# Opening of a windowed-attention and MLP-mixer kernel: loads in smaller pieces, earlier casting DMAs, wider zero matmuls, another mask on TensorE

## The chip, the cores and the metric

The kernel runs on one core of a Trainium2 chip. The metric is the device time of one execution in microseconds. Its engines run beside each other, each with its own queue: TensorE (PE; its weight loads are listed apart as PEld), VectorE (DVE), ScalarE (ACT), GpSimd (POOL) and SyncE (SP), which here only issues DMAs. Sixteen DMA engines move the data of all queues.

## What is computed

The input is q, k and v of 4 batches with 8 heads, 768 positions and 64 channels per head. Attention sees the first 4 positions (the sinks) and a window of 128; the result goes through a mixer of two small networks, one over positions ("token") and one over channels.

```
scores = scale * (q @ k^T);  pos = arange(S);  rel = pos[:, None] - pos[None, :]
keep = (pos[None, :] < n_sink) | ((rel >= 0) & (rel < window))        # 4 and 128
scores = where(keep, scores, -1e9);  a = softmax(scores);  x = a @ v   # heads side by side: [4, 768, 512]
h = relu(x^T @ w_tok1) @ w_tok2                                       # over the 768 positions
u = x + h^T
out = u + relu(u @ w_ch1) @ w_ch2                                     # 512 -> 1536 -> 512 channels
```

## The kernel before

The work is cut into operations (`Op`), each with the engines that may do it, an estimated duration, and what it depends on. A planner, `order_of`, puts them in order with a list-scheduling rule, and each engine's instructions are emitted in that order. For the opening the order is written out by hand in `FIRST`: each word is an operation and its engine (`:P` TensorE, `:D` VectorE, `:A` ScalarE, `:G` GpSimd, `:S` SyncE). Every engine works its own list strictly in order and waits where its next instruction's inputs are missing.

There are eight groups, each of four heads of one batch. A group goes through these steps:

- **L, load.** Group 0's q and k come as fp32 by SyncE's DMAs (`plain`, L355) in `PIECES[0]` pieces each, and are cast to bf16 by ScalarE or VectorE (`C`, L234). All later groups' q and k come by GpSimd's DMAs, which cast on the way (`casting`, L363). v comes by SyncE (L373) and is cast later (`Cv`, L232 or L233).
- **T, turn.** VectorE transposes q and k in 32x32 blocks (L395).
- **SC, scores** (L447). A block `u` of 256 keys (three per group) against up to 512 queries. For groups 0 and 1 two heads go together, each on 32 rows of the array, into one of two PSUM slots of two banks (kind "sc").
- **EX, exponentials** by ScalarE from PSUM (L464), which frees the slot.
- **MK, mask.** VectorE multiplies by 0 and 1 (L475, with `mfirst` and `mrest`), except for the (group, block) pairs in `PEM`: there TensorE first writes -30000 where a key is not seen (`ident` times `mneg`, L440) and adds the scores onto it.
- **KZ, SK, EXK.** The sink keys, spread over heads with `blk`, their scores (L501) and exponentials (L506).
- **PV** (L520 for the sinks, L523 and L528 for the window) and **XB** (L543, L544: divide by the sum).

Once both groups of a batch are through, the mixer follows: T1 (L572, needs `w_tok1`), H1, TT and T2 (L603 to L624), U, X, C1 (L657), V, C2 (L679) and the output's addition and store (L689, L694). While C1 and C2 of one batch run, the planner mixes in the next batch's attention.

The weights come by GpSimd's DMA queue, in a fixed sequence; the first of them, w_tok1, is not issued before group 0's v has landed. The queue also carries the sink rows of v (`vsl`, L307) and waits for earlier DMAs when eight are under way.

Where the planner sees a gap before a TensorE operation, `Filler.make` puts matmuls of zeros there, up to 29 us of its own time: at the very start matmuls of 512 columns over 128 rows (L791), in later gaps matmuls of 128 columns, over 32 rows ahead of scores (L793), over 128 rows otherwise.

Of the kernel before, what the change touches and what calls it, by code (L numbers as in the profile page):

```python
# [16 lines left out]


FIRST = """
warm:D ones:D va:G Lk0.1:S kz:D Lq0.0:S blk:G Lk0.0:S zero:D vsink:A ident:G Lq0.1:S Lv0.0:S mneg:G Lv1.0:S  # L20
Lv1.1:S Ck0.1:A Lk1.0:G mnegs:D Tk0.1:D Lq1.0:G Cq0.0:A vs1:G Tq0.0:D Ck0.0:A vsl:G Tk0.0:D Cq0.1:A Tq0.1:D
first:G KZ0:D SC0.22:P rest:G first1:D SK0:P EX0.21:A Tk1.0:D SC0.20:P SC0.10:P EX0.20:A EX0.10:A SC0.12:P
MK0.20:D EX0.11:A SC0.02:P KZ1:D Tq1.0:D EXK0:A SC0.00:P Wtok1:G EX0.01:A Wtok2:G EX0.00:A Cv0:D SC1.00:P
SK1:P Wch1.0:G EX1.00:A MK0.10:D PV0.5:P PV0.1:P Wch1.1:G PV0.0:P EXK1:A SC1.02:P XB0.5:D Cv1:G SC1.12:P
EX1.01:A XB0.0:D PV0.4:P XB0.1:D PV0.2:P EX1.11:A Wch1.2:G XB0.4:D SC1.10:P PV0.3:P MK1.00:D EX1.10:A Wch1.3:G
SC1.20:P XB0.2:D Wch2.0:G XB0.3:D SC1.22:P EX1.20:A MK1.0256:D Wch2.1:G T10.010:P EX1.21:A MK1.10:D PV1.0:P
PV1.1:P T10.000:P T10.004:P XB1.0:D PV1.2:P H10.00:A PV1.3:P PV1.4:P XB1.2:D PV1.5:P T10.014:P XB1.4:D
T10.110:P H10.01:A T10.100:P T10.104:P T10.114:P H10.10:D TT0.01:P H10.11:D TT0.00:P UE0.01:A TT0.02:P
UE0.00:A TT0.03:P UE0.02:A UE0.03:A C10.03:P C10.02:P V0.03:A C10.00:P V0.02:D C10.01:P V0.00:D V0.01:D
"""  # L30


# [7 lines left out]
class Op:  # L40


    n = 0
# [23 lines left out]
def order_of(ops, slots, filler):  # L67

    free_at = {e: 0.8 for e in ("PE", "ACT", "DVE", "POOL", "SP")}
    banks = {kind: [0.0] * n for kind, n in slots.items()}  # L70
    dma_free, rows = {"SP": 1.9, "POOL": 6.0, "ACT": 1.9}, None
    port = 0.0
    flying = {"SP": [0.0] * 8, "POOL": [0.0] * 8}
    flying["ACT"] = flying["SP"]
    for o in reversed(sorted(ops, key=lambda o: o.seq)):
        for d in o.deps:
            d.far = max(d.far, o.far + min(o.engines.values()) + (0.2 if "PE" in d.engines else 0.07))
    waiting = sorted(ops, key=lambda o: o.seq)
    done = []

    def start(op, e):
        t = free_at[e]
        for d in op.deps:
            t = max(t, d.end + lag(d, op, e))
        for d in op.follows:
            t = max(t, d.begin + d.engines[d.engine])
        if op.take:
            for kind in {p.kind for p in op.take}:
                n = sum(p.kind == kind for p in op.take)
                t = max(t, sorted(banks[kind])[n - 1])  # L90
        if op.dmas:
            t = max(t, flying[e][-9 + op.dmas])
        if e in op.port:
            t = max(t, port)
        if e == "PE" and op.rows != rows:
            t += 0.095
        return t

    while waiting:
        best = None  # L100
        ready = [o for o in waiting if all(d.end is not None for d in o.deps + o.follows)]
        per = {}
        for o in ready:
            at = {e: start(o, e) for e in o.engines}
            soonest = min(at[e] + o.engines[e] + o.dear.get(e, 0) for e in at)
            for e, t in at.items():
                if t < INF and t + o.engines[e] + o.dear.get(e, 0) <= soonest + 1e-9:
                    per.setdefault(e, []).append((t, o))
        for e, c in per.items():
            first = min(t for t, _ in c)  # L110
            t, o = min(((t, o) for t, o in c if t <= first + 0.2), key=lambda x: (x[1].pri, -x[1].far, x[1].seq))
            if best is None or t < best[0]:
                best = (t, e, o)
        if best is None:
            raise RuntimeError("stuck: " + ", ".join(o.name for o in waiting[:20]))
        t, e, o = best
        idle = t - free_at["PE"] - (1.0 if rows is None else 0.15)
        kind, i = min(((k, i) for k in banks for i in range(slots[k])), key=lambda x: banks[x[0]][x[1]])
        if e == "PE" and filler.until > t and idle > 0.15 and banks[kind][i] < free_at["PE"] - 0.2:
            f = filler.make(kind, i, idle, rows is None, o.rows)  # L120
            f.begin, f.engine = free_at["PE"], "PE"
            f.end = banks[kind][i] = f.begin + f.engines["PE"]
            done.append(f)
        o.begin, o.engine = t, e
        free_at[e] = t + o.engines[e]
        if e in o.port:
            port = free_at[e]
        if e == "PE":
            rows = o.rows
        if o.land:  # L130
            dma_free[e] = max(dma_free[e], t + (2.8 if e == "POOL" else 1.4)) + o.land
            o.end = dma_free[e] + 0.9
            flying[e] += [o.end] * o.dmas
        else:
            o.end = free_at[e]
        for p in o.take:
            p.slot = min(range(len(banks[p.kind])), key=lambda i: banks[p.kind][i])
            banks[p.kind][p.slot] = INF
        for p in o.free:
            p.left -= 1  # L140
            if p.left == 0:
                banks[p.kind][p.slot] = free_at[e] + 0.07
        done.append(o)
        waiting.remove(o)
    return done
# [11 lines left out]
def kernel(  # L157
# [13 lines left out]
    nc = tc.nc  # L171
    B, H, S, D = q.shape
    P = 128
# [13 lines left out]
    Q = 32  # L187
# [21 lines left out]
    ident = singles.tile([P, P], BF16, name="ident")  # L209
# [15 lines left out]
    def op(name, engines, emit, deps=(), pri=0, **kw):  # L225
        if not isinstance(engines, dict):
            engines = dict([engines])
        o = Op(name, engines, emit, deps, pri, **kw)
        ops.append(o)
        return o  # L230
# [46 lines left out]
    def c_masks(m):  # L277
        def emit(e):
            z = m.rearrange("p (x c q) -> p x c q", c=2, q=P)
            causal(nc.gpsimd, z[:, :, 0], 0.0)  # L280
            behind(nc.gpsimd, z[:, :, 1], 0.0)
        return emit
# [41 lines left out]
        pass  # L324

    groups = [Group() for _ in range(NG)]
    PEM = ((0, 0), (1, 2))
    PIECES = (2, 1, 1, 1, 1, 1, 1, 1)
    PAIRS = (1,)
    BW, BWV = 0.37, 0.25  # L330

    def behind_of(ins, o):

# [47 lines left out]
    def attention(g, xb, base):  # L381
        G = groups[g]
# [7 lines left out]
        def turn(w, c):  # L390
            def emit(e):
                if w not in G.T:
                    G.T[w] = att.tile([P, S, 2], BF16, name=w + "T")
                r = ts(c, S // Q // C)
                nc.vector.transpose(  # L395
                    G.T[w].rearrange("p s x -> p (s x)").bitcast(UINT32).rearrange("p (i r) -> p r i", i=Q)[:, r],
                    G.bf[w][:, r].bitcast(UINT32))
            old = (prev.sc + [prev.sk]) if prev else []
            return op(f"T{w}{g}.{c}", ("DVE", 2.0 / C + 0.1), emit, G.load[w][c:c + 1] + old, early + c)

        dts = {"q": [], "k": []}
        for c in range(C):
# [309 lines left out]

    o_warm = op("warm", ("DVE", 0.27), c_warm, (), -200)
    o_table = op("table", ("ACT", 1.4), c_table, [o_warm], -60)
    c_ident_op = op("ident", ("POOL", 1.1), c_ident, (), -200)
    o_zero = op("zero", ("DVE", 0.5), c_zero, (), -199)
    o_mneg = op("mneg", ("POOL", 1.4), c_mneg, [o_zero], -199)
    c_mneg_op = op("mnegs", ("DVE", 0.17), c_mneg_sink, [o_mneg], -199)
# [6 lines left out]
    load_ops(0, [], [], -250)  # L725
    load_ops(1, [], [], -180)
    for o in groups[1].load["q"] + groups[1].load["k"]:
        o.deps += [c_ident_op, o_mneg, c_blk_op]
    o_vs1 = op("vs1", ("POOL", 0.9), c_vsink_one, [o_vs], -151)
    c_vsink_op = op("vsl", ("POOL", 2.6), c_vsink_load, [o_vs1], -150, land=2.0)  # L730
    c_vsink_op.dmas = 4
    o_first = op("first", ("POOL", 0.65), c_masks(mfirst), [o_ones], -120)
    c_first_op = op("first1", ("DVE", 0.17), c_mfirst_sink, [o_first], -120)
    c_rest_op = op("rest", ("POOL", 0.65), c_masks(mrest), [o_ones], -119)

    def weight(key, dst, src, deps, pri, run):

# [40 lines left out]
    class Filler:  # L778
# [2 lines left out]
        until = 29.0  # L781

        @staticmethod
        def make(kind, i, us, first, rows):
            n = int(us / 0.33) if first else int(us / 0.058)

            def emit(e):
                t = psum[kind][i].tile([P, 512], FP32, name="ps_warm", tag="b")
                for _ in range(n):
                    if first:  # L790
                        nc.tensor.matmul(t, warm[:, 0:P], warm, start=True, stop=True)  # L791
                    elif rows:
                        nc.tensor.matmul(t[:, 0:P], warm[0:Q, 0:P], warm[0:Q, 0:P], start=True, stop=True, tile_position=(0, 0))  # L793
                    else:
                        nc.tensor.matmul(t[:, 0:P], warm[:, 0:P], warm[:, 0:P], start=True, stop=True)
            return Op("dummy", {"PE": us}, emit)

    with tc.manual_schedule():
# [35 lines left out]
```

## Time and profile before

| | us |
|---|---|
| median of 8 runs | 220.37 |
| fastest and slowest of them | 219.42, 221.60 |
| the profiled execution | 220.16 |
| its span, first to last instruction | 218.5 |
| TensorE busy | 205.8 (94%) |
| VectorE busy | 127.8 (58%) |
| ScalarE busy | 107.1 (49%) |
| GpSimd busy | 32.4 (15%) |

The span starts with the first instruction. The page's chain is the sequence of work and waits that ended last, followed back from the end; the idle time of an engine is put down to what released it, inferred from semaphores. The page also has a row of 40 slices for each engine, of 5.46 us each, with the clock that TensorE was granted and the share of the DMA engines:

```profile
PE   7799999999889699999989999999999999999994
ACT  8485733733856224788652330598553301753300
PEclk9965999999999999999999999999999999999999
DMA  6999999999999955540000112200001112101122
```

The first digit of each row is the slice from 0 to 5.46 us; 9 means nine tenths or more. The costliest groups are the mixer's matmuls (columns: line, engine, operation, tiles, shapes and count, then busy time and mean in ns, then idle time of the engine before them):

```profile
L657 PE MATMUL ps_v<-uT,w_ch 128*128 128x384 bf16 x384 | 68.2, 326 | 0.4
L679 PE MATMUL ps_w<-w_ch,v 128*128 128x512 bf16 (+1 forms) x288 | 64.7, 370 | 0.6
L464 ACT ACTIVATE pT<-ps_s 128x1024 bf16<-128x1024 f32 (+1 forms) x48 | 43.6, 952 | 26.4 <-PE ps_s L447 24.7
L447 PE MATMUL ps_s<-qT,kT 32*128 32x256 bf16 (+1 forms) x384 | 20.4, 279 | 2.3 <-DVE kz L419 1.6
```

### The profile page before, as it was taken

The page shows a single profiled execution, that of the slowest core. Times are in us where ns is not written, and L with a number is a line of the kernel's source. Part 1 is how long each engine was busy: PE and PEld are TensorE (multiplying, and loading weights), DVE is VectorE, ACT ScalarE, POOL GpSimd, SP SyncE. Part 2 cuts the span into 40 slices and gives each one's busy share as a digit, 9 for nine tenths or more (in the row PEclk, how much of TensorE's full clock was granted, in tenths as well). Part 3 has the DMA queues.
Part 4 walks back from the last instruction along what each step waited for, and adds up shares of the span by engine and source line. Part 5 has one row for each costly group of instructions (what it writes and reads, how often), then busy time and mean ns, then how long its engine had stood idle before and what let it go on. Part 6 is the DMA issues. An engine that isn't in the chain of part 4 may idle for free.

```text
span 218.5 us, 4156 instructions
## 1 busy us (share of the span) xinstructions
PE 205.8 (94%) x1748; PEld 117.9 (54%) x1767; DVE 127.8 (58%) x227; ACT 107.1 (49%) x176; POOL 32.4 (15%) x54
## 2 busy tenths in 40 slices
PE   7799999999889699999989999999999999999994
PEld 2346685655455465565735554466665545655543
DVE  4767865199698998989999212588471122001132
ACT  8485733733856224788652330598553301753300
POOL 7709700002633030111000000000000000000000
PEclk9965999999999999999999999999999999999999
DMA  6999999999999955540000112200001112101122
GB/s 200 249 220 175 202 203 200 208 231 218 216 221 252 233 145 117 104 91 0 3 0 0 51 48 96 98 3 3 0 3 48 48 48 99 48 1 48 48 99 96
DMA packets 36243, 23.89 MB, mean 109 GB/s; under 512 B 26112, under 2 KB 30976, under 8 KB 36224
## 3 DMA queue, kind: packets, MB, share of 16 engines
q1 hardware_dynamic: 28896, 14.16, 26.0%
q0 software_dynamic: 7328, 9.46, 25.0%
q8 instruction: 14, 0.23, 0.4%
q14 instruction: 5, 0.04, 0.1%
HBM read 26.77 MB, written 6.29 MB: 151 GB/s over the span
## 4 chain that ended last, share of the span: by engine, by line
PE 77%; DVE 10%; DMA 6%; ACT 3%; issue 2%; SPq 1%; POOLq 0%; POOL 0%
PE ps_v L657 26%; PE ps_w L679 26%; PE ps_s L447 6%; PE ps_u L624 5%; PE ps_h L572 4%; DVE pT L475 3%; DMA qb<-in_q_dram 3%; DMA raw_q<-in_q_dram 3%; DVE x_b L544 3%; DVE qT L395 2%; ACT pT L464 2%; PE ps_ut L634 2%; PE ps_k L501 2%; PE ps_o L523 2%; PE ps_o L520 2%
## 5 line engine op out<-in xcount | busy, mean ns | idle before, releaser
L657 PE MATMUL ps_v<-uT,w_ch 128*128 128x384 bf16 x384 | 68.2, 326 | 0.4
L238 ACT ACTIVATE v<-ps_v 128x384 bf16<-128x384 f32 x85 | 41.4, 494 | 50.8 <-PE ps_v L657 40.0
L679 PE MATMUL ps_w<-w_ch,v 128*128 128x512 bf16 (+1 forms) x288 | 64.7, 370 | 0.6
L464 ACT ACTIVATE pT<-ps_s 128x1024 bf16<-128x1024 f32 (+1 forms) x48 | 43.6, 952 | 26.4 <-PE ps_s L447 24.7
L689 DVE TENSOR_TENSOR o<-ps_w,u_sb 128x512 f32<-128x512 f32 (+1 forms) x25 | 16.7, 672 | 59.2 <-PE ps_w L679 59.2
L657 PEld LDWEIGHTS <-w_ch 128*128 128x128 bf16 x384 | 36.4, 98 | 25.6 <-DVE x_b L544 0.8
L679 PEld LDWEIGHTS <-v 128*128 128x128 bf16 x300 | 28.8, 98 | 30.2 <-issue 0.4
L475 DVE TENSOR_TENSOR pT<-pT,mrest 128x2048 bf16<-128x2048 bf16 (+2 forms) x22 | 22.2, 1021 | 0.9 <-ACT pT L464 0.7
L447 PE MATMUL ps_s<-qT,kT 32*128 32x256 bf16 (+1 forms) x384 | 20.4, 279 | 2.3 <-DVE kz L419 1.6
L629 DVE TENSOR_TENSOR u_sb<-ps_u,x_b 128x512 bf16<-128x512 f32 x24 | 15.2, 684 | 9.6 <-PE ps_v L657 5.1
L544 DVE TENSOR_TENSOR x_b<-ps_o,rc 128x256 bf16<-128x256 f32 (+1 forms) x45 | 19.9, 442 | 1.6
L395 DVE STREAM_TRANSPOSE kT<-kb 128x768 uint32<-128x768 uint32 (+1 forms) x9 | 16.8, 1870 | 3.6 <-DMA kb<-in_k_dram 2.3
L447 PEld LDWEIGHTS <-kT 32*128 32x128 bf16 x384 | 11.1, 97 | 12.4 <-issue 9.7
L523 PE MATMUL ps_o<-va,pT 128*128 128x65 bf16 x192 | 16.8, 197 | 1.1 <-DVE v L240 0.8
L395 DVE STREAM_TRANSPOSE qT<-qb 128x768 uint32<-128x768 uint32 (+1 forms) x9 | 16.6, 1871 | 1.2 <-DMA qb<-in_q_dram 0.9
L233 POOL CAST va<-raw_v 128x1536 bf16<-128x1536 f32 x7 | 10.7, 1523 | 44.2 <-DMA raw_v<-in_v_dram 22.5
L523 PEld LDWEIGHTS <-pT 128*128 128x128 bf16 x192 | 14.3, 100 | 2.5 <-DVE pT L475 0.8
L528 PE MATMUL ps_o<-va,pT 128*128 128x65 bf16 x160 | 15.2, 196 | 0.0
L234 ACT ACTIVATE uT<-ps_ut 128x512 bf16<-128x512 bf16 (+1 forms) x14 | 7.9, 567 | 10.0 <-PE ps_ut L634 8.3
L572 PE MATMUL ps_h<-x_b,w_tok 128*128 128x256 bf16 x96 | 12.3, 273 | 0.2 <-DVE x_b L544 0.2
L624 PE MATMUL ps_u<-h,w_tok 128*128 128x512 bf16 x44 | 12.2, 378 | 0.3 <-ACT uT L234 0.2
L528 PEld LDWEIGHTS <-pT 128*128 128x128 bf16 x160 | 11.6, 100 | 0.8 <-issue 0.4
(63 smaller groups left out, 135.9 us busy)
## 6 DMA issues: line engine op xcount, KB each, us to landing
out_dram<-o SPq DMA_DIRECT2D x23, 256.0 KB, 2.0
raw_v<-in_v_dram SPq DMA_DIRECT2D x7, 768.0 KB, 12.9
kb<-in_k_dram POOLq DMA_DIRECT2D x7, 384.0 KB, 11.4
qb<-in_q_dram POOLq DMA_DIRECT2D x7, 384.0 KB, 9.3
w_ch<-in_moe_w_ch_dram POOLq DMA_DIRECT2D x4, 384.0 KB, 8.5
w_ch<-in_moe_w_ch_dram POOLq DMA_DIRECT2D x1, 1024.0 KB, 14.4
raw_k<-in_k_dram SPq DMA_DIRECT2D x2, 384.0 KB, 4.3
raw_q<-in_q_dram SPq DMA_DIRECT2D x2, 384.0 KB, 5.0
```

The lines of the kernel that those rows point to most:

```text
L238: nc.scalar.activation(o, i, AF.Relu)
L395: nc.vector.transpose(G.T[w].rearrange("p s x -> p (s x)").bitcast(UINT32).rearrange("p (i r) -> p r i", i=Q)[:, r], G.bf[w][:, r].bitcast ...
L447: nc.tensor.matmul(bank[h][:, at:at + w], G.T["k"][r, ts(kt, P), db], G.T["q"][r, ds(kt * P, w), db], start=not pem and db == 0, stop=db = ...
L464: nc.scalar.activation(o, i, AF.Exp, scale=scale)
L475: nc.vector.tensor_tensor(out=t, in0=t, op=ALU.mult, in1=m[:, 0:hi - lo].rearrange("p (o x) -> p o x", o=1).to_broadcast([P, GH, hi - lo]))
L523: nc.tensor.matmul(ps[:, h], G.pT[qt // 2][:, h, ds(256 * (qt % 2), P)], G.va[:, h, qt], start=(qt < 2 and h == 0), stop=(h == GH - 1 and ...
L528: nc.tensor.matmul(ps[:, h], G.pT[kt // 2][:, h, ds(256 * (kt % 2) + P, P)], G.va[:, h, kt], start=False, stop=(h == GH - 1), skip_group_c ...
L544: nc.vector.tensor_tensor(out=xb.tile[:, ds(q0, n), c0:c0 + W].rearrange("p n (h d) -> p n h d", h=GH), in0=ps[:, :, :, 0:D], in1=rc.to_br ...
L572: nc.tensor.matmul(p.tile, w_tok1[:, t, ts(tt, P)], xb.tile[:, t, ds(a * W, W)], start=(t == 0), stop=(t == NT - 1))
L624: nc.tensor.matmul(ps, w_tok2[:, tt, ts(st, P)], M.h1t[:, tt], start=(tt == 0), stop=(tt == NTOK - 1))
L657: nc.tensor.matmul(ps, w_ch1[:, c, ts(ft, P)], M.uT[hf][:, c], start=(c == 0), stop=(c == NC - 1))
L679: nc.tensor.matmul(p.tile, M.v1t[hf][:, ft, ts(st % NH, P)], w_ch2[:, ft, ds(lo, n)], start=(ft == 0), stop=(ft == NF - 1))
```

## The change

It has five parts.

1. Group 0's q and k come in three pieces each, six DMAs of 256 KB where there were four of 384 KB (`PIECES`). The new order loads and casts q's last piece first; that first cast is VectorE's, the other five are ScalarE's.
2. Group 1's two casting DMAs no longer wait for `mneg`. They stand third in GpSimd's list, after `ident` and `blk`, and q goes ahead of k; `mneg` now follows them, and `va`, `vs1`, `first` and `rest` follow `mneg`.
3. The zero matmuls ahead of the first scores are counted anew (29 where there were 24), and those in later gaps have 256 columns over 128 rows; `idle` is measured with other margins.
4. `PEM` gets the pair (0, 1): group 0's second block is masked by TensorE too, so two of its three blocks are.
5. The planner's figures for the DMA queues, the transposes, `ident` and the load rate are altered, and `FIRST` is written anew with the score blocks of group 0 in another sequence (heads 2 and 3 of all three blocks, then heads 0 and 1). Through the planner this also moves later work: eight C1 matmuls now stand ahead of group 2's scores, and group 4's q is turned after group 3's attention rather than within it.

```diff
 FIRST = """
-warm:D ones:D va:G Lk0.1:S kz:D Lq0.0:S blk:G Lk0.0:S zero:D vsink:A ident:G Lq0.1:S Lv0.0:S mneg:G Lv1.0:S
-Lv1.1:S Ck0.1:A Lk1.0:G mnegs:D Tk0.1:D Lq1.0:G Cq0.0:A vs1:G Tq0.0:D Ck0.0:A vsl:G Tk0.0:D Cq0.1:A Tq0.1:D
-first:G KZ0:D SC0.22:P rest:G first1:D SK0:P EX0.21:A Tk1.0:D SC0.20:P SC0.10:P EX0.20:A EX0.10:A SC0.12:P
-MK0.20:D EX0.11:A SC0.02:P KZ1:D Tq1.0:D EXK0:A SC0.00:P Wtok1:G EX0.01:A Wtok2:G EX0.00:A Cv0:D SC1.00:P
...
+warm:D ident:G Lq0.2:S ones:D vsink:A Lk0.1:S blk:G kz:D Lq0.1:S zero:D Lq1.0:G Lk0.2:S Lk1.0:G Lq0.0:S mneg:G
+Lk0.0:S Lv0.0:S Cq0.2:D Lv1.1:S Tq0.2:D va:G Lv1.0:S Ck0.1:A vs1:G mnegs:D Tk0.1:D Cq0.1:A first:G Ck0.2:A
+Tq0.1:D rest:G Cq0.0:A Tk0.2:D vsl:G Ck0.0:A Tq0.0:D Tk0.0:D KZ0:D SC0.22:P first1:D SC0.12:P EX0.21:A Tq1.0:D
+SC0.02:P EX0.11:A SK0:P EX0.01:A Tk1.0:D SC0.20:P EX0.20:A SC0.00:P EXK0:A SC0.10:P KZ1:D EX0.00:A Cv0:D
+Wtok1:G SK1:P Wtok2:G EX0.10:A MK0.20:D PV0.1:P SC1.02:P Wch1.0:G XB0.1:D EXK1:A SC1.00:P EX1.01:A PV0.0:P
...
-    dma_free, rows = {"SP": 1.9, "POOL": 6.0, "ACT": 1.9}, None
+    dma_free, rows = {"SP": 2.1, "POOL": 6.9, "ACT": 2.1}, None
...
-        idle = t - free_at["PE"] - (1.0 if rows is None else 0.15)
+        idle = t - free_at["PE"] - (0.0 if rows is None else 0.1)
-        if e == "PE" and filler.until > t and idle > 0.15 and banks[kind][i] < free_at["PE"] - 0.2:
-            f = filler.make(kind, i, idle, rows is None, o.rows)
+        if e == "PE" and filler.until > t and idle > 0.2 and banks[kind][i] < free_at["PE"] - 0.2:
+            f = filler.make(kind, i, idle, rows is None)
...
+            t = max(t, f.end + 0.095 * o.rows)
-            dma_free[e] = max(dma_free[e], t + (2.8 if e == "POOL" else 1.4)) + o.land
+            dma_free[e] = max(dma_free[e], t + (3.3 if e == "POOL" else 1.4)) + o.land
...
-    PEM = ((0, 0), (1, 2))
-    PIECES = (2, 1, 1, 1, 1, 1, 1, 1)
+    PEM = ((0, 0), (0, 1), (1, 2))
+    PIECES = (3, 1, 1, 1, 1, 1, 1, 1)
-    BW, BWV = 0.37, 0.25
+    BW, BWV = 0.35, 0.25
...
-            return op(f"T{w}{g}.{c}", ("DVE", 2.0 / C + 0.1), emit, G.load[w][c:c + 1] + old, early + c)
+            return op(f"T{w}{g}.{c}", ("DVE", 1.96 / C + 0.16), emit, G.load[w][c:c + 1] + old, early + c)
...
-    c_ident_op = op("ident", ("POOL", 1.1), c_ident, (), -200)
+    c_ident_op = op("ident", ("POOL", 0.5), c_ident, (), -200)
...
-        o.deps += [c_ident_op, o_mneg, c_blk_op]
+        o.deps += [c_ident_op, c_blk_op]
+    o_mneg.follows = list(groups[1].load["k"])
...
+    for o in (c_va_op, o_vs1, o_first):
+        o.follows = [o_mneg]
+    c_rest_op.follows = [o_mneg]
...
-            n = int(us / 0.33) if first else int(us / 0.058)
+            n, w = (11 + int((us - 4.8) / 0.216), 512) if first else (round(us / 0.11), 256)
...
-                    if first:
-                        nc.tensor.matmul(t, warm[:, 0:P], warm, start=True, stop=True)
-                    elif rows:
-                        nc.tensor.matmul(t[:, 0:P], warm[0:Q, 0:P], warm[0:Q, 0:P], start=True, stop=True, tile_position=(0, 0))
-                    else:
-                        nc.tensor.matmul(t[:, 0:P], warm[:, 0:P], warm[:, 0:P], start=True, stop=True)
+                    nc.tensor.matmul(t[:, 0:w], warm[:, 0:P], warm[:, 0:w], start=True, stop=True)
```

More of the change, by code (lines that the diff above doesn't have):

```diff
@@ L19 @@
 FIRST = """
-warm:D ones:D va:G Lk0.1:S kz:D Lq0.0:S blk:G Lk0.0:S zero:D vsink:A ident:G Lq0.1:S Lv0.0:S mneg:G Lv1.0:S
-Lv1.1:S Ck0.1:A Lk1.0:G mnegs:D Tk0.1:D Lq1.0:G Cq0.0:A vs1:G Tq0.0:D Ck0.0:A vsl:G Tk0.0:D Cq0.1:A Tq0.1:D
-first:G KZ0:D SC0.22:P rest:G first1:D SK0:P EX0.21:A Tk1.0:D SC0.20:P SC0.10:P EX0.20:A EX0.10:A SC0.12:P
-MK0.20:D EX0.11:A SC0.02:P KZ1:D Tq1.0:D EXK0:A SC0.00:P Wtok1:G EX0.01:A Wtok2:G EX0.00:A Cv0:D SC1.00:P
[L24 to L29, printed above, removed]
+warm:D ident:G Lq0.2:S ones:D vsink:A Lk0.1:S blk:G kz:D Lq0.1:S zero:D Lq1.0:G Lk0.2:S Lk1.0:G Lq0.0:S mneg:G
[3 more added lines that the diff above has]
+Wtok1:G SK1:P Wtok2:G EX0.10:A MK0.20:D PV0.1:P SC1.02:P Wch1.0:G XB0.1:D EXK1:A SC1.00:P EX1.01:A PV0.0:P
+Wch1.1:G PV0.4:P XB0.0:D PV0.2:P XB0.4:D EX1.00:A Cv1:G SC1.10:P XB0.2:D PV0.3:P EX1.10:A SC1.12:P XB0.3:D
+Wch1.2:G PV0.5:P MK1.0256:D EX1.11:A SC1.22:P Wch1.3:G XB0.5:D SC1.20:P MK1.00:D Wch2.0:G EX1.21:A MK1.10:D
+T10.000:P Wch2.1:G EX1.20:A PV1.0:P PV1.1:P T10.004:P XB1.0:D PV1.2:P H10.00:A PV1.3:P PV1.4:P XB1.2:D PV1.5:P
+T10.010:P XB1.4:D T10.100:P T10.014:P T10.110:P H10.01:A T10.114:P T10.104:P H10.11:A TT0.00:P H10.10:A
+TT0.01:P UE0.00:D TT0.02:P UE0.01:A TT0.03:P UE0.02:A UE0.03:A C10.03:P C10.00:P V0.03:D C10.01:P V0.00:D
+C10.02:P V0.01:D V0.02:D
 """
@@ L783, in make @@
         @staticmethod
-        def make(kind, i, us, first, rows):
-            n = int(us / 0.33) if first else int(us / 0.058)
+        def make(kind, i, us, first):
+            n, w = (11 + int((us - 4.8) / 0.216), 512) if first else (round(us / 0.11), 256)
             def emit(e):
```

## The prediction

> **What bounds the kernel now.** I read the page first (busy shares, the slices, the chain), then stretches of the span, then the timelines of ScalarE, GpSimd and VectorE over the opening, then the DMA queues by stretch. The page has TensorE busy for 94% of the span and on 77% of the chain, so a microsecond in which TensorE is slow or waits is a microsecond of the kernel. The exception is its clock: the slices show tenths "9965999", so I cut the opening where the granted clock changes (columns: stretch, its length, busy time and instructions of TensorE, its weight loads, VectorE, ScalarE, GpSimd, then clock, DMA share, GB/s):
>
> ```profile
> 5.86:9.27 3.41, 3.00 (x14) 1.26 (x13) 2.45 (x4) 1.82 (x3) 3.33 (x9) 1.00 1.09 269
> 9.27:12.68 3.41, 2.24 (x32) 1.53 (x32) 1.37 (x3) 1.49 (x2) 0.62 (x2) 1.00 1.16 217
> 12.68:16.10 3.42, 3.00 (x28) 1.37 (x26) 3.16 (x4) 2.77 (x5) 0.24 (x1) 0.50 1.23 223
> 16.10:19.51 3.41, 3.41 (x25) 1.82 (x24) 3.41 (x3) 2.03 (x3) 3.41 (x4) 0.50 1.20 169
> 19.51:22.92 3.41, 3.41 (x37) 2.40 (x37) 2.01 (x7) 1.72 (x3) 3.41 (x5) 0.50 1.22 194
> 22.92:26.34 3.42, 3.42 (x57) 2.05 (x53) 2.52 (x8) 3.07 (x4) 2.85 (x5) 1.00 1.31 203
> ```
>
> The clock is halved from 12.68 to 22.92 us, and in these 10.24 us ScalarE, which makes the exponentials, is busy 6.52 us. Its timeline (start, duration, line, tiles, idle time before and its releaser) shows that it waits for TensorE's scores each time:
>
> ```profile
> 8.38 0.84 ACT L234 ACTIVATE qb<-raw_q 128x768 bf16<-128x768 f32 x1 [0.59 <-DMA raw_q<-in_q_dram]
> 10.99 0.81 ACT L464 ACTIVATE pT<-ps_s 128x768 bf16<-128x768 f32 x1 [1.77 <-PE ps_s L447]
> 15.89 1.02 ACT L464 ACTIVATE pT<-ps_s 128x1024 bf16<-128x1024 f32 x1 [0.44 <-PE ps_s L447]
> 17.82 1.02 ACT L464 ACTIVATE pT<-ps_s 128x1024 bf16<-128x1024 f32 x1 [0.91 <-PE ps_s L447]
> 19.31 1.02 ACT L464 ACTIVATE pT<-ps_s 128x1024 bf16<-128x1024 f32 x1 [0.47 <-PE ps_s L447]
> 22.56 3.10 ACT L464 ACTIVATE pT<-ps_s 128x1024 bf16<-128x1024 f32 x3 [1.69 <-PE ps_s L447]
> 25.87 1.69 ACT L464 ACTIVATE pT<-ps_s 128x768 bf16<-128x768 f32 x2 [0.20 <-PE ps_s L447]
> ```
>
> Groups 0 and 1 need four exponentials of 0.81, eight of 1.02 and two of 0.59: 12.6 us. They take from 10.99 to 27.56, 16.6 us; 4.0 us are stalls. After them TensorE is dense: from its first token-mixing matmul (L572, 26.71) to 54.94 it loses about 0.2 us. So the opening is a chain of three: the first q and k, the scores at half clock, the exponentials. The DMA engines are full from 2 to 78 us, yet the weights land before use (first token weight at 21.79, used at 26.71). The chain has one more stall that the change touches:
>
> ```profile
> 59.78 7.24 DMA qb<-in_q_dram
> 67.05 2.09 DVE qT L395
> ```
>
> Here VectorE waits 0.9 us for a later group's q, then turns it, in the middle of group 3's masks.
>
> [...] Weighing each matmul by its columns and its share of the 128 rows, I get 0.30 of full work in 9.27 to 12.68 (clock lost), 0.55 and 0.55 in the next two (not regained), 0.72 in 19.51 to 22.92 (regained); later windows at 0.50 (from 70.7) and 0.53 (from 74.1) keep it. So it is lost somewhere between 0.30 and 0.50, and regained between 0.55 and 0.72. [...] these two stretches (6 to 8.6 us, then 10.5 to 12.5 us) show: once GpSimd's queue has data, both send the same number of packets, 138 and 136, and its large ones take 96% of the engines.
>
> ```profile
> q1 hardware_dynamic: 1534, 0.74, 102.3%
> ...
> q0 software_dynamic: 138, 0.38, 96.1%
> q1 hardware_dynamic: 136, 0.03, 12.6%
> ```
>
> **The change part by part.**
>
> Six pieces. The last 384 KB piece lands at 8.35; then come its cast (0.84), its transpose (1.13) and 0.12 of hand-over: scores at 10.44. With 256 KB the cast is about 0.63 (two thirds of 768 columns and the fixed part) and the transpose 0.82 (0.94 per 12 rows from the forms 1.13 and 2.07, plus 0.19), so the scores follow the landing by 1.6, not 2.09. Two more DMA issues at 0.43 each put the v loads back by 0.9 us in SP's queue; they share the engines with the end of q and k from 6.9 us on now, so that helps slightly. If the last piece still lands near 8.35, the scores can start at 9.95.
>
> Casting DMAs third. They leave GpSimd at about 2.2 us, after ident (0.5) and blk (0.8), not at 4.11. When do they move data? Before, their first packet came at 8.74, 4.6 us after the issue; later single issues on an empty queue took 1.25 (80.33 to 81.58). Bounds for the first packet: 3.5 to 6.8 us. At 6.8 only some 5 of the 48 raw packets per DMA engine are left and each waits for one casting packet of 0.25 us: 1.2 us, landing near 8.4 because v no longer mixes in. I take this, since the 4.6 us is the only first use of that queue in the trace. Group 1's q and k then land near 11 and 12.5 (before: 14.98 and 12.91), their two transposes (2.07) end by about 15.2, not 17.89. The moved GpSimd work (mneg 1.3, va 0.4, vsink 0.9, masks 1.4, four sink DMAs 2.4) ends at about 10 as before; mneg is ready at 4.7, the sinks' DMAs queue behind the casts as before. First v is behind the same bytes: still about 15.5, so w_tok1, which waits for it, still lands near 21.5.
>
> Wide zero matmuls. The opening run grows from 24 to 29. With the clock raised at 5.86, 10.8 run at 0.427 us and 18.2 at 0.216: it ends at 9.8, where the scores start. If the window falls at 8.1 it ends at 10.9, if at 4.7 at 9.2: on average 0.2 us lost. The 19 small ones (L793, a quarter of the rows) go; only one gap of two 256-wide ones is left in the new order.
>
> Masks on TensorE. Group 0's second block: four matmuls of 0.213 at full clock replace VectorE's 1.21 us multiply. TensorE is ahead of ScalarE there, so they cost nothing, unless the clock is down (0.427 each).
>
> The sum, engine by engine, at full clock. Scores 9.9; exponentials from 10.45. Two score banks alternate, each score block (0.45, with a mask 0.9) fits beside an exponential of 1.02: u2 ends at 11.26, u1 12.42, u0 13.44, u2 14.25, sinks 14.84, u0 15.86, u1 16.88. Group 1's keys are ready at 15.3, so its sink scores go at 15.6. The first PV waits for v cast on VectorE (15.6 to 16.6), and group 1's scores stand behind it in TensorE's order: at 17.0, for an exponential that can start at 17.5. Then 0.59 and six exponentials: 23.3. The first L572 matmul goes when the last score block is out, at 22.4, where w_tok1 has landed 0.9 us before. Before: 26.71. Gain 4.3, minus 0.2 for the window's phase.
>
> The window rule on this schedule: about 0.70, 0.61, 0.51 and 0.63 of full work from 9.27 to 22.92. The third is the weak one, at the edge of what was seen to hold.
>
> After 22.4. The new order puts eight first-channel matmuls (1.3 us) ahead of group 2's scores and takes nothing else out, so these come at 52.0, not 54.94. Group 2's k lands at 46.5 and its transpose ends by 48.7; v is cast at 52.4 and used from 55.6: covered by 3 us. Group 4's q is now turned after group 3's attention: at most 1.8 us of TensorE idle time between 66 and 78 goes, but VectorE, nearly full from 57 to 118, gets the 2.09 back before group 4. I take 0.3 of gain (bounds 1.5 gain, 1.0 loss, since the order of three later groups shifts as well).
>
> Profiled run: 220.16 (span 218.5 and 1.7 outside) minus 4.1 minus 0.3 is 215.8. The median is 0.2 above that run: 216.0.
>
> **Rivals.**
>
> *Half the gain.* One of the weak windows falls under the clock's limit, or loads and VectorE take some back between 52 and 118. For: the third window at 0.51, and VectorE at 3.7 to 4.0 of every 4 us from 86 to 114. Against: loads have 3 us to spare. A window of 3.4 us at half clock costs about 2: 218.2.
>
> *Nothing.* All of it is met by the DMA engines, which are full to 78 us: what lands late then holds group 2 and 3. Against: q, k, v of these are used 3 us or more after landing. 220.2.
>
> *Slower: the casting DMAs overtake the first loads.* Place: the DMA engines, 3.5 to 8 us. If their first packet comes before about 5.1 us, at least 16 raw packets per engine are still to go, and all 16 casting packets (0.246 each) step between: 3.9 us more, last piece at 11.3, scores at 12.9. The zero matmuls end at 9.8, so the window to 12.7 holds under 0.2 of full work and the clock goes. Masked score blocks at half clock take 1.7, 0.7 more than an exponential; with one such window the exponentials end at 28.1, with two at 30, against 27.56. That is 221 to 223, say 222. It decides from a landing of about 10.4 us on. For: single issues had data after 1.25 us. Against: the 4.6 us at this very place.
>
> **How the numbers follow.** Full gain 0.50 (own range 214.3 to 217.6), half 0.21, nothing 0.10, slower 0.19. What a measurement of this kernel can tell from no change is about 0.5%, that is 219.3 to 221.5. Full and half are faster, 0.71, with a little of "nothing" 0.72; same 0.10; slower 0.18, as a mild case of the last falls within. The range from 214.3 to 221.2 leaves out some 0.05 below and 0.15 above.
>
> **What would show it.** Right: last raw piece landing by 8.6; first exponential at 10.5; a clock of 1.00 from 6 us on; ScalarE without stalls over 0.3 us to 23; first L572 at 22 to 23; group 2's scores near 52. Wrong: casting packets before 5 us and a raw landing past 10; a half clock anywhere before 23; a first L572 after 25; VectorE or TensorE idle time over 7 us after it.

## The result, and the profile after

The kernel after takes 222.65 us (median of 11 runs, 221.04 to 223.34); the kernel before, timed beside it, 220.34 (32 runs). The ratio is 1.009, 95% interval 1.0065 to 1.0115: 0.9% slower, a small loss but clear of the interval, where 216.0 was forecast. Here and below, ratios leave disturbed executions out and medians don't, so some medians (x4, x9) lie above what their ratios say. The profiled execution took 221.08, its span 219.4, against 218.5 before.

First the opening, cut where the granted clock changes (columns: stretch, length, busy time and count of TensorE, weight loads, VectorE, ScalarE, GpSimd, then clock, DMA share, GB/s):

```profile
6.15:9.56 3.41, 3.41 (x17) 1.53 (x16) 1.59 (x4) 0.63 (x1) 3.27 (x7) 1.00 1.08 249
9.56:12.98 3.42, 0.53 (x3) 0.04 (x1) 1.83 (x3) 1.89 (x3) 0.00 (x0) 1.00 1.20 258
12.98:16.39 3.41, 2.73 (x19) 1.02 (x20) 3.38 (x5) 0.81 (x1) 0.00 (x0) 0.50 1.36 211
16.39:19.80 3.41, 3.07 (x21) 1.06 (x20) 2.62 (x3) 2.05 (x2) 3.23 (x4) 0.50 1.07 151
19.80:23.22 3.42, 3.42 (x20) 0.98 (x14) 1.36 (x1) 2.05 (x3) 3.42 (x5) 0.50 1.27 200
23.22:26.63 3.41, 3.41 (x59) 2.38 (x60) 1.26 (x5) 2.93 (x5) 3.03 (x5) 1.00 1.32 204
```

In the second stretch TensorE has work for 0.53 of 3.42 us, and three stretches of 3.41 us at half clock follow, as before; such a stretch is called a window here and in the prediction. In both traces the granted clock changes a whole number of windows behind the moment at which the zero matmuls begin to follow each other in 0.22 us instead of 0.43: after at 12.98, 23.22 and 217.78 us, behind 6.15; before at 12.68, 22.92 and 217.48, behind 5.86. TensorE's timeline says what it waited for (start, duration, line, tiles, idle time before and its releaser):

```profile
1.26 8.83 PE L796 MATMUL ps_warm<-warm 128*128 128x512 bf16 x29 [1.26 <-DVE warm L256]
13.66 0.82 PE L449 MATMUL ps_s<-qT,kT 32*128 32x256 bf16 x8 [3.57 <-DVE kT L397]
```

The zero matmuls end at 10.09, and the first scores stand 3.57 us behind them, waiting for the last piece of k. ScalarE's timeline follows k back to its DMA and on to the exponentials:

```profile
7.75 0.63 ACT L236 ACTIVATE qb<-raw_q 128x512 bf16<-128x512 f32 x1 [2.92 <-DMA raw_q<-in_q_dram]
10.31 0.63 ACT L236 ACTIVATE kb<-raw_k 128x512 bf16<-128x512 f32 x1 [1.93 <-DMA raw_k<-in_k_dram]
11.23 0.63 ACT L236 ACTIVATE qb<-raw_q 128x512 bf16<-128x512 f32 x1 [0.30 <-DMA raw_q<-in_q_dram]
12.13 0.63 ACT L236 ACTIVATE kb<-raw_k 128x512 bf16<-128x512 f32 x1 [0.26 <-DMA raw_k<-in_k_dram]
14.52 0.81 ACT L466 ACTIVATE pT<-ps_s 128x768 bf16<-128x768 f32 x1 [1.76 <-PE ps_s L449]
16.45 1.02 ACT L466 ACTIVATE pT<-ps_s 128x1024 bf16<-128x1024 f32 x1 [1.12 <-PE ps_s L449]
18.39 1.02 ACT L466 ACTIVATE pT<-ps_s 128x1024 bf16<-128x1024 f32 x1 [0.91 <-PE ps_s L449]
```

The last raw piece lands at 12.10 us; before, at 8.35. The first exponential is 3.5 us later (14.52, before 10.99), and the stalls of half clock are still there (1.12, 0.91). The DMA queues from 6 to 8.6 us, the stretch that before held SyncE's packets alone (queue, packets, MB, share of 16 engines):

```profile
q0 software_dynamic: 141, 0.39, 77.0%
q1 hardware_dynamic: 136, 0.25, 29.9%
```

GpSimd's queue sends packet for packet with SyncE's (141 and 136), and its packets, 0.23 us each against 0.09, take 77% of the engines just while q and k of group 0 should come in. Its first packet moves at 4.94 us.

The loss shrinks later. The first token-mixing matmul (T1 below: L574, L572 before) starts at 30.24 us, 3.6 later than before (26.64), but the span is only 0.9 longer: from T1 to the end it takes 189.2 us instead of 191.9. Group 4's q is now turned at 79.51, without a wait. The slices and the costliest groups hardly differ:

```profile
PE   7859999999989999989999999999999999999993
ACT  7236874353496613698744730496553301753300
PEclk9965899999999999999999999999999999999998
DMA  6999999999999916391000012200001113001122
```

```profile
L466 ACT ACTIVATE pT<-ps_s 128x1024 bf16<-128x1024 f32 (+1 forms) x48 | 43.8, 953 | 14.3 <-PE ps_s L449 12.2
...
L449 PE MATMUL ps_s<-qT,kT 32*128 32x256 bf16 (+1 forms) x384 | 20.0, 276 | 4.6 <-DVE kT L397 3.6
```

In the slices the half clock reaches further into the fifth one. Of the groups one number is new: the 3.6 us in which TensorE waited for `kT`. ScalarE's idle time before its window exponentials fell from 26.4 to 14.3 us, but most of that only moved: 10.4 us now stand before the sinks' exponentials (L508), where there were none.

### The profile page after: what moved, and what is told of

Read it like the earlier page. It is cut to its first block, busy times and chain, and to the rows that moved or that the text cites. A ratio compares the mean times of both kernels' runs of the same rounds, so it can differ in the third digit from the quotient of the medians.

```text
span 219.4 us, 4147 instructions
## 1 busy us (share of the span) xinstructions
PE 206.2 (94%) x1738; PEld 116.7 (53%) x1759; DVE 128.0 (58%) x229; ACT 107.3 (49%) x177; POOL 31.7 (14%) x54
## 4 chain that ended last, share of the span: by engine, by line
PE 85%; DMA 4%; DVE 4%; ACT 3%; issue 2%; SPq 1%; ACTq 0%
PE ps_w L681 28%; PE ps_v L659 28%; PE ps_s L449 8%; PE ps_h L574 5%; PE ps_u L626 5%; DMA raw_k<-in_k_dram 4%; PE ps_o L525 2%; PE ps_s L442 2%; PE ps_o L522 2%; PE ps_ut L636 2%; ACT pT L466 2%; PE ps_o L530 2%; DVE pT L477 1%; DVE x_b L546 1%; PE ps_k L503 1%
## 5 line engine op out<-in xcount | busy, mean ns | idle before, releaser
L240 ACT ACTIVATE v<-ps_v 128x384 bf16<-128x384 f32 x87 | 42.6, 493 | 50.0 <-PE ps_v L659 39.0
L466 ACT ACTIVATE pT<-ps_s 128x1024 bf16<-128x1024 f32 (+1 forms) x48 | 43.8, 953 | 14.3 <-PE ps_s L449 12.2
L477 DVE TENSOR_TENSOR pT<-pT,mrest 128x1536 bf16<-128x1536 bf16 (+2 forms) x21 | 20.4, 972 | 3.5 <-ACT pT L466 3.4
L449 PEld LDWEIGHTS <-kT 32*128 32x128 bf16 x384 | 10.4, 96 | 17.0 <-issue 10.5
L525 PE MATMUL ps_o<-va,pT 128*128 128x65 bf16 x192 | 16.3, 194 | 0.4 <-DVE v L242 0.3
L530 PE MATMUL ps_o<-va,pT 128*128 128x65 bf16 x160 | 14.8, 193 | 0.0
L525 PEld LDWEIGHTS <-pT 128*128 128x128 bf16 x192 | 13.5, 98 | 2.0 <-DVE o L691 0.5
L574 PE MATMUL ps_h<-x_b,w_tok 128*128 128x256 bf16 x96 | 12.0, 273 | 0.0
L530 PEld LDWEIGHTS <-pT 128*128 128x128 bf16 x160 | 11.3, 98 | 1.0 <-issue 0.4
L236 ACT ACTIVATE uT<-ps_ut 128x512 bf16<-128x512 bf16 (+1 forms) x13 | 7.3, 571 | 7.9 <-PE ps_ut L636 7.3
## 6 DMA issues: line engine op xcount, KB each, us to landing
kb<-in_k_dram POOLq DMA_DIRECT2D x7, 384.0 KB, 10.4
```

The lines of the kernel that those rows point to most:

```text
L240: nc.scalar.activation(o, i, AF.Relu)
L449: nc.tensor.matmul(bank[h][:, at:at + w], G.T["k"][r, ts(kt, P), db], G.T["q"][r, ds(kt * P, w), db], start=not pem and db == 0, stop=db = ...
L466: nc.scalar.activation(o, i, AF.Exp, scale=scale)
L477: nc.vector.tensor_tensor(out=t, in0=t, op=ALU.mult, in1=m[:, 0:hi - lo].rearrange("p (o x) -> p o x", o=1).to_broadcast([P, GH, hi - lo]))
L525: nc.tensor.matmul(ps[:, h], G.pT[qt // 2][:, h, ds(256 * (qt % 2), P)], G.va[:, h, qt], start=(qt < 2 and h == 0), stop=(h == GH - 1 and ...
L530: nc.tensor.matmul(ps[:, h], G.pT[kt // 2][:, h, ds(256 * (kt % 2) + P, P)], G.va[:, h, kt], start=False, stop=(h == GH - 1), skip_group_c ...
```

## The experiments

All eleven experiments, with the moments that the text uses (us; each ratio is to the kernel before as timed beside that run: its median was 220.63 for x1 to x7, 219.98 for x8 to x11, 220.34 for after; T1 is the first token-mixing matmul of the profiled execution, the last column its span less T1):

| run | median | ratio to before, 95% | last raw piece | first exponential | T1 | span less T1 |
|---|---|---|---|---|---|---|
| before | 220.34 | | 8.35 | 10.99 | 26.64 | 191.9 |
| after | 222.65 | 1.0090 (1.0065 to 1.0115) | 12.10 | 14.52 | 30.24 | 189.2 |
| x1 | 217.13 | 0.9825 (0.9765 to 0.9885) | 8.39 | 10.50 | 25.11 | 190.3 |
| x2 | 218.97 | 0.9937 (0.9915 to 0.9959) | 13.48 | 15.59 | 27.80 | 189.6 |
| x3 | 222.07 | 1.0101 (1.0044 to 1.0157) | 10.14 | 12.78 | 28.23 | 190.6 |
| x4 | 220.79 | 0.9953 (0.9913 to 0.9994) | 8.17 | 10.80 | 28.96 | 192.4 |
| x5 | 219.81 | 0.9956 (0.9934 to 0.9977) | 8.53 | 11.17 | 24.33 | 194.0 |
| x6 | 218.24 | 0.9894 (0.9833 to 0.9955) | 8.66 | 11.29 | 24.40 | 192.0 |
| x7 | 221.55 | 1.0037 (1.0005 to 1.0070) | 8.54 | 10.65 | 23.73 | 195.8 |
| x8 | 215.47 | 0.9791 (0.9774 to 0.9809) | 8.25 | 10.46 | 24.20 | 189.9 |
| x9 | 218.90 | 0.9848 (0.9800 to 0.9896) | 8.16 | 10.87 | 24.74 | 189.2 |
| x10 | 215.04 | 0.9786 (0.9759 to 0.9812) | 8.61 | 11.25 | 24.31 | 188.8 |
| x11 | 224.73 | 1.0206 (1.0186 to 1.0227) | 13.11 | 15.53 | 32.60 | 190.5 |

### Do the casting DMAs make the loss? (x1, x3)

x1 is the kernel after with these two DMAs issued behind `mneg`; x3 is the kernel before with them issued third. In both, each engine's order is otherwise kept by moving the operations in the finished plan:

```diff
-        for o in order_of(ops, slots, Filler):
+        plan = order_of(ops, slots, Filler)
+        casts = [o for o in plan if o.name in ('Lq1.0', 'Lk1.0')]
+        plan = [o for o in plan if o not in casts]
+        at = 1 + [o.name for o in plan].index('mneg')        # x3: 'ident'
+        plan[at:at] = casts
+        for o in plan:
             o.emit(o.engine)
```

> The changed kernel with one edit: group 1's two casting DMAs stand behind mneg in GpSimd's list again, all other engines' orders are those of the changed kernel. Theory 1 (the casting packets overtake the first loads, the rest of the change is sound): the issue goes from 2.1 to about 4.2 us, the first casting packet from 4.94 to 7.1 or later, the last raw piece lands between 8.0 and 9.3 (12.10 in the changed kernel), first scores between 9.8 and 10.9 (13.66), first token matmul between 22.5 and 25 (30.31), 216 to 218 us. Rival (the six pieces, the new order or the masks cost the time themselves): the landing moves, but the time stays at 221 us or more.

> The kernel before with one edit: its two casting DMAs stand third, after blk and ident and ahead of mneg, pieces and all else as before. Theory 1: the first casting packet comes near 5.3 us (8.74 before), the last raw piece of 384 KB lands at 11 to 12 (8.35 before), first scores near 13.5 (10.44), 222 to 224 us. Rival (only small pieces are overtaken, or the casting queue has no data before some 7 us unless something else in the change lets it): landing under 9.5, time within 219.5 to 221.5.

x1 gives 217.13 us: 5.5 below after, 3.5 below before timed beside it. Its casting packets begin at 8.19 (issue at 4.10) and the last raw piece lands at 8.39. ScalarE's cast of that piece, and the DMA queues from 6 to 8.6 us, now read

```profile
8.41 0.63 ACT L236 ACTIVATE kb<-raw_k 128x512 bf16<-128x512 f32 x1 [0.22 <-DMA raw_k<-in_k_dram]
```

```profile
q1 hardware_dynamic: 1807, 0.73, 106.3%
q0 software_dynamic: 9, 0.03, 5.4%
```

x3 loses what after lost (ratio 1.010), though its first casting packet came only at 6.08 and its last piece landed at 10.14, 1.8 us later than before and short of the 11 to 12 expected. The DMAs' place alone makes after slow; without that the rest of the change is a gain.

### How much of it is the clock? (x2, x8)

x2 is after with 46 zero matmuls ahead of the first scores in place of 29.

> The changed kernel with 46 zero matmuls ahead of the first scores in place of 29, so that they end near 13.6 us, where its scores start. Raw pieces still land at about 12. Theory 1a (of the 3.6 us lost at the first token matmul, most is the half clock that the idle window brings): the clock stays up from 6 us on, the exponentials end near 27 and the first token matmul comes at 26 to 27 (30.31), the time is 218.5 to 220. Rival (the lateness of the loads alone counts, ScalarE is not held up by the clock): first token matmul after 29, time 221.5 or more.

Its raw piece landed even later (13.48), but the clock stayed up from 6.04 us on, T1 came at 27.80 (26 to 27 was expected) and it took 218.97: so the half clock is some 3.7 us of after's time. A late landing under a full clock still costs 3.5 against x8 below. x8 is x1 with zero matmuls in two gaps that x1's TensorE timeline shows:

```profile
16.87 0.62 PE L503 MATMUL ps_k<-qT,kz 128*128 128x512 bf16 x2 [0.80 <-DVE kz L421]
18.08 0.19 PE L525 MATMUL ps_o<-va,pT 128*128 128x65 bf16 x1 [0.58 <-DVE va L234]
```

```diff
+        gaps = {'SK1': 0.8, 'PV0.1': 0.6}
         for o in plan:
+            if o.name in gaps:
+                Filler.make('mx', o.take[0].slot, gaps[o.name], False).emit(None)
             o.emit(o.engine)
```

> The version at 217.13 us (after, its casting DMAs behind mneg) with seven 256-wide zero matmuls more ahead of group 1's sink scores and five ahead of the first PV, the two places where its TensorE waited 0.80 and 0.58 us and its clock fell in 18.5 to 21.9 us. Theory (that one window of half clock costs about 1.8 us, as the single run of that version at a clock of 1.0 suggests with 215.33): clock at 1.0 until the last slice, 215.2 to 216.3 us. Rival (what the window costs is met by later waits): 216.8 to 217.5.

In x8 the same place reads

```profile
15.96 0.94 PE L796 MATMUL ps_warm<-warm 128*128 128x256 bf16 x7
17.15 0.62 PE L503 MATMUL ps_k<-qT,kz 128*128 128x512 bf16 x2 [0.25 <-DVE kz L421]
17.61 0.71 PE L796 MATMUL ps_warm<-warm 128*128 128x256 bf16 x5
```

and all five runs had a clock of 0.999 or 1.0: 215.47 us, within the theory's range. A window at half clock costs some 1.7 us there. That is no fixed price: x9's profiled execution, below, lost a window from 16.97 to 20.38 and still took 215.57.

### Where does an opening's gain go? (x4 to x7, x11)

The prediction let what is won at T1 reach the end. In the kernel before, though, VectorE turns group 4's q ahead of group 3's masks and of group 2's last two divisions (the prediction and the texts below place it in the middle of those masks). That q lands at about 67 us whatever the opening did (67.03 in before, 67.41 in after, 66.85 in x5, 66.71 in x7). In before, GpSimd issues it at 59.78, behind the cast of a v that lands at 57.87, and on full DMA engines (share 1.20 from 59.78 to 67.05) it takes 7.24 us. x4 is before with that turn (and the load that it releases) behind group 3's attention; x5 is before with wide zero matmuls alone; x6 has both; x7 is x1 with the turn put back.

```diff
+        moved = [o for o in plan if o.name in ('Tq4.0', 'Lq6.0')]
+        plan = [o for o in plan if o not in moved]
+        at = 1 + [o.name for o in plan].index('O0.30')       # x4, x6; x7, x11: 'XB2.3'
+        plan[at:at] = moved
```

```diff
-            n = int(us / 0.33) if first else int(us / 0.058)
+            n, w = (31, 512) if first else (round(us / 0.11), 256)   # x5, x6; the matmuls as in after
```

> The kernel before, with one step moved: group 4's q turn (and the load that it releases) behind group 3's attention. Nothing of the opening changes. Theory A (before, VectorE stands in the middle of group 3's masks until group 4's q lands at 67 us, and this wall takes back what an opening gains): 217.5 to 219.5 us, and TensorE's idle time between 60 and 80 us falls by 1 us or more. Theory B (the wait there costs nothing, as TensorE has other work): 219.8 to 221.

> The kernel before, with the zero matmuls alone changed: 31 wide ones ahead of the first scores, 256 columns wide over all rows in each later gap. The clock should stay up through the opening and the first token-mixing matmul come at 24 to 25 us instead of 26.6. Theory A (the wall at 67 us takes the gain back): 219.3 to 221 us. Theory B (what is gained at that matmul reaches the end one for one, as the prediction assumed): 217 to 218.7.

> Both edits to the kernel before: the wide zero matmuls, and group 4's q turn behind group 3's attention. Theory A: the two give more together than the sum of each alone, 215.5 to 217.5 us. Theory B: no more than the zero matmuls alone, 217 to 218.7.

> The kernel after with its two casting DMAs issued behind mneg (the run at 217.13), and group 4's q turn put back to where the kernel before has it, in the middle of group 3's masks. Theory A (the wall at 67 us): 218.5 to 220.5 us, TensorE idle 1 us or more longer between 60 and 80 us. Theory B (the place of that turn does not matter): 216.5 to 218.

x5 is the clearest. The clock stayed up and T1 came 2.3 us earlier (24.33), yet it took 219.81 us, 0.4% less than before. VectorE's line for group 4's q, first in x5, then in x7, against 0.90 us of waiting in before:

```profile
66.85 2.09 DVE L395 STREAM_TRANSPOSE qT<-qb 128x768 uint32<-128x768 uint32 x1 [2.96 <-DMA qb<-in_q_dram]
```

```profile
66.71 2.09 DVE L397 STREAM_TRANSPOSE qT<-qb 128x768 uint32<-128x768 uint32 x1 [3.38 <-DMA qb<-in_q_dram]
```

The earlier VectorE arrives, the longer it waits: 2.06 us more in x5 for 2.3 us won. In x7 TensorE runs dry behind it, and its clock falls once more (granted 0.83 from 68 to 72 us, 0.74 from 72 to 76):

```profile
64.94 0.63 PE L449 MATMUL ps_s<-qT,kT 32*128 32x256 bf16 x16
69.37 0.81 PE L574 MATMUL ps_h<-x_b,w_tok 128*128 128x256 bf16 x5 [3.80 <-DVE o L691]
```

x7's 221.55 against x1's 217.13 is the price of that one step with an early opening: 4.4 us, with the windows at half clock that it costs; between executions of either with one such window it is 3.6 (220.72 and 217.13). Both are more than theory A allowed. With the zero matmuls and the turn moved (x6), before comes to 218.24, above theory A's range and within theory B's. By the ratios it is 1.1% below before, about the sum of x4's and x5's gains (0.5% and 0.4%), not more than it as theory A had it; the table below says otherwise.

The runs also differ among themselves in how many windows of 3.41 us they spend at half clock, each of which lowers the mean granted clock by 0.008. Medians by that count, with the number of runs (after with one more than its median has; other counts, 17 runs of before and one of x4, left out):

| half-clock windows | none | 1 | 3 | 4 | 5 |
|---|---|---|---|---|---|
| before | 219.99 (9) | 219.94 (5) | 220.06 (33) | 220.71 (14) | 221.70 (11) |
| x4 | 217.61 (2) | | 220.43 (9) | 223.09 (4) | 222.93 (4) |
| x2 | 218.90 (16) | 220.51 (4) | | | |
| after | | | 221.53 (4) | 222.73 (6) | 223.56 (2) |
| x11 | | | | 223.85 (1) | 224.80 (3) |

In before, three such windows cost nothing: the time won by a full clock is spent waiting at 67 us. From the fourth on they do cost. With the turn moved (x4) the same three cost 2.8 us, though only two runs had none. x4's median lies above theory A's range and in theory B's because 18 of its 20 runs had three windows or more; over all 20 it is no faster than before (220.79 to 220.63). Measured from before at three windows (220.06), the turn alone at three gives nothing (220.43), the zero matmuls alone some 0.25 (x5, 219.81), both together 1.8 (x6): by this count the two do give more together than the sum, as the wall at 67 us would have it.

x11 is the kernel after with the turn put back.

> The kernel after, only group 4's q turn put back into the middle of group 3's masks, as the kernel before has it. Theory A with the late opening of after (first token-mixing matmul at 30.2 us, so VectorE comes to that turn about when q4 lands at 67.4): the wall costs 0 to 1 us, 222.6 to 223.6. Rival (that order costs its 4 us whatever the opening): 225 to 227.

Its T1 came at 32.60 in the profile, so VectorE reached the turn at 71.59, after q4's landing, and waited for nothing. At the same count of windows it is 1.1 to 1.2 us slower than after (four runs). So even without the wait the turn stands badly there, as 2.07 us of VectorE ahead of group 3's masks.

The turn is not all that the new order brings behind T1. x6 has the turn late, a full clock and T1 at 24.40, and takes 192.0 us from there; x8, also with the turn late, a full clock and T1 at 24.20, takes 189.9, x10 188.8, with the same matmuls behind T1. So some 2 to 3 us there come from the rest of the new order, which no experiment takes apart.

x11's time lies above the expected 222.6 to 223.6, as T1 was later than reckoned (32.60 for 30.2) and all four runs had four or five windows at half clock.

### What do the other parts bring? (x9, x10)

x9 is x1 without the second mask on TensorE (VectorE multiplies ahead of PV0.1 instead); x10 is x1 with q and k in four pieces of 12 rows instead of six of 8.

```diff
-                if pem:
+                pe_mask = pem and (g, u) != (0, 1)     # x9
+                if pe_mask:
...
+                src = heads(q if w == "q" else k, g).rearrange("h (i r) d -> (h i) r d", i=Q)[:, ts(c2, 12)]   # x10
```

> The version at 217.13 us without the second mask on TensorE: group 0's second block is multiplied by VectorE ahead of the first PV, four mask matmuls fewer (0.85 us of TensorE work in the opening). Prediction's view (the mask matmuls stand beside exponentials and cost or bring nothing by themselves): 216.6 to 217.8. Rival (they are part of what keeps the clock up): the windows from 11.6 and 15.1 us lose about 0.12 of full work each, one window more at half clock, 218 to 219.5. Third: VectorE's 1.2 us multiply stands ahead of the first XB and delays group 1's scores, T1 0.5 to 1.2 us later at an unchanged clock, 217.6 to 218.3.

> The version at 217.13 us with group 0's q and k in four pieces of 384 KB instead of six of 256 KB, every engine's order otherwise kept. Prediction's step (six pieces bring the first scores 0.5 us forward, 10.4 to 9.9 us): first scores 0.3 to 0.6 us later than 9.95, time 0.2 to 0.6 us longer, 217.3 to 217.8. Rival (the number of pieces does not matter, the landing of the last byte does): first scores within 0.15 us of 9.95 and 216.8 to 217.3.

x9's runs spread from 215.57 to 221.66: two of six at a clock of 0.992 or more, three at 0.976, one at 0.969. With a full clock it took 216.06 in its only such run, beside 215.47 in x8. The mask matmuls cost nothing that shows. Only two of x9's six runs had at most one window at half clock, of x1 and x10 nine of ten, and x9's median lies in the rival's range (218 to 219.5). That leans to the rival, by which these matmuls hold the clock; six runs don't settle it.

x10 contradicts the prediction's step. Its first scores are 0.74 us later than x1's (10.69), as four pieces should make them, but it is no slower: 215.04 us, the lowest of all (x8's interval overlaps), five of six runs at full clock. In x10 group 1's sink scores still wait for that group's k:

```profile
17.56 0.62 PE L511 MATMUL ps_k<-qT,kz 128*128 128x512 bf16 x2 [0.74 <-DVE kz L429]
```

What the scores win early is lost by the first PV, which also waits for the cast of v: it goes at 18.54, in x8 at 18.42. T1 is at 24.31, in x8 at 24.20.

## Why the prediction was wrong

**The step that failed** is "When do they move data?": of bounds from 3.5 to 6.8 us it took 6.8, because the queue's only first use in the trace of before had lagged its issue by 4.6 us. The first packet came at 4.94. With that the term "1.2 us, landing near 8.4" becomes 3.7 us more, landing at 12.10. From there on the prediction's own rival took over: it named this place, a decision point of 5.1 us, a landing at 11.3, scores at 12.9 and 222 us; measured 12.10, 13.66 and 222.65. x1 and x3 show the cause from both sides. The mechanism was seen and the wrong end of an unknown cost was taken: one lag, seen with other work ahead of it on GpSimd, was no ground to prefer the late bound. That the rival's 222 came so close is in part luck: it counted one or two windows at half clock where there were three, and none of the 2.7 us that came back behind T1.

**The zero matmuls and the clock.** The run ended at 10.09 (9.8 was reckoned), which no longer reached the scores. The limits read from before held in after: at 0.06 of full work (9.56 to 12.98) the clock fell, and it came back at 0.75 (19.80 to 23.22). The weak third window, reckoned at 0.51, held 0.34 in x1, where the landing was as predicted, and lost the clock too.

**The sum to 22.4.** Even with a landing as predicted and a full clock, T1 came at 24.20 (x8). The term behind it: group 1's k was to land at about 12.5, which needs the early casts; with late ones it lands at 14.76, and the sink scores go at 17.15, not 15.6. The early casts and the early first scores draw on the same DMA time (k at 11.82 and scores at 13.66 in after, 14.76 and 9.90 in x8); the sum booked both.

**Six pieces.** The 0.5 us at the first scores is real (9.95 in x1, exactly as worked out; 10.69 in x10, of which 0.2 is a later landing), its worth at T1 is 0.1 us at most (x10 beside x8).

**The mask matmuls at no cost.** No cost shows, though few runs of x9 kept the clock; that the masks bring something, by holding it, stays open.

**After T1.** "I take 0.3 of gain (bounds 1.5 gain, 1.0 loss)" was mis-sized. Its cost was right: group 2's scores follow T1 by 29.58 us, by 28.23 before, the 1.3 us of eight matmuls. In the traces span less T1 shrinks by 2.7 us from before to after, which hides most of the 3.6 us lost before it. The prediction saw VectorE's 0.9 us wait for group 4's q, but took it as a fixed price; it is a wall in absolute time, and after's late opening comes to it too late to wait. To have the turn there costs 1.1 us behind after's late opening (x11) and 4.4 behind x1's early one (x7). The rest of the new order is worth 2 to 3 us there (x8 and x10 beside x6), for which the prediction booked 0.3 in all; which part of it does so stays open. By the same wall, "a microsecond in which TensorE is slow or waits is a microsecond of the kernel" was false for before: its three windows at half clock cost nothing.

Together: plus 3.6 at T1 (minus 4.3 was forecast), minus 2.7 after it (minus 0.3), plus 0.9 for the profiled executions. The medians lie 2.3 apart, as the profiled execution of after had three windows at half clock and the median run four.

## What to carry to other kernels

A transfer started early on an idle queue was not free here, where another queue was loading what came first: its packets took 77% of the DMA engines from 6 to 8.6 us, and the last raw piece landed at 12.10 us, where it landed at 8.39 with the same transfer issued later (x1, 4.10 us for 2.08). Count what such packets take, and if their start is unknown, price both ends before choosing. Before valuing a saving, look downstream for an engine that, in its own order, waits for something landing at a fixed time, as VectorE did for group 4's q (67.03 us in before, 66.85 in x5, 66.71 in x7): of the 2.3 us won in x5, 2.06 went into that wait, and to move the waiting instruction was worth 4.4 us (x1 beside x7). Zero matmuls had to reach the first real one at its latest arrival, not its likely one: 17 more gave back some 3.7 us here (x2).

## What was not expected of the hardware

From the issue of the first casting DMA to its first packet it took 2.2 to 2.9 us in the three kernels with after's early issue (x2, x11, after), 3.7 in x3 and 3.9 to 4.9 in the nine others, where the issue came at 4.1 to 4.4 us. What sets this wasn't tried.

VectorE's cast of q's first piece (128x512) took 0.43 us in x7, x8 and x9, but 1.80 in after, 1.69 in x2 and 1.86 in x11, where GpSimd had issued its casting DMAs just before (at 2.08 and 2.74 in after; in x8 the first at 4.29). Both lines, after first, then x8:

```profile
3.50 1.80 DVE L234 CAST qb<-raw_q 128x512 bf16<-128x512 f32 x1 [0.66 <-DMA raw_q<-in_q_dram]
```

```profile
3.42 0.43 DVE L234 CAST qb<-raw_q 128x512 bf16<-128x512 f32 x1 [0.58 <-DMA raw_q<-in_q_dram]
```

In x1, with its first issue at 4.10, it took 0.90. What stretched the cast is not shown. In after it put the next transpose back by some 0.9 us against x1 (5.34, 4.46); the transposes still ended ahead of the late landings, so this cost nothing.

In the openings the clock was lost after windows with 0.06 (after), 0.19 (x3), 0.27 (x4), 0.30 (before), 0.31 (x11) and 0.34 (x1, x9) of full work (weighed as in the prediction) and kept after 0.34 in x2 and x5, so 0.34 went both ways; at half clock it stayed down at 0.71 (x4) and 0.719 (x11) and came back at 0.725 (before) and above.
